# Adding the query halves in the transfer, with pair two's remainders on other engines, fewer dummy matmuls and a new order

## The chip, the cores and the metric

The kernel runs on one core of a Trainium2 chip. The metric is the device time in microseconds of one execution; the median of several runs is compared. Traces are of one profiled execution. The engines are TensorE (PE; its weight loads are PEld), VectorE (DVE), ScalarE (ACT), GpSimd (POOL) and SyncE (SP, which only issues transfers here).

## What is computed

Attention with pooled queries, then a layer of eight experts with a capacity. All inputs and outputs are float32.

```python
def _attn_ref(q, k, v):                      # q, k, v: (8, 8, 1152, 64)
    q_pool = q.reshape(B, H, S // 2, 2, D).mean(axis=3)
    scores = scale * np.matmul(q_pool, k.transpose(0, 1, 3, 2))
    scores = scores - np.max(scores, axis=-1, keepdims=True)
    attn = np.exp(scores)
    attn = attn / (np.sum(attn, axis=-1, keepdims=True) + 1e-09)
    return np.matmul(attn, v)

# x = the 4608 x 512 attention result; logits = x @ w_gate (512 x 8)
# the logits are taken in falling order: a token goes to the expert if it has none yet
# and the expert has fewer than 4608 / 8 = 576 tokens
    h = np.maximum(x[mask] @ w1[e], 0.0)
    out[mask] = h @ w2[e]
```

## The kernel before

**Work and stages.** `attention()` (line 355 on) works on 32 pairs of heads, 0 to 31. A pair has 18 steps: nine blocks of 128 keys for each of its two heads. It is followed by `experts()` (line 966 on), which the change leaves alone. The 576 queries of a head are the sums of two neighbours, so the queries come as two halves of 128 x 576 numbers (both heads of a pair on the 128 partitions), which have to be added.

**A pair's preparation.** `load` (L484) has SP fetch both query halves into QD (576 KB) and the keys into KD in two parts; `load_v` (L492) fetches VD. `split` (L557) adds the halves into QS on VectorE (L561), and makes of the scaled float32 numbers two float16 numbers each, a high part and a remainder: QH and QL of the queries, KH and KL of the keys. `values` (L615) does the same for V, into V16. ScalarE writes the high parts; VectorE writes the remainders (QL L583, KL L596, V L631), each in one instruction that scales and subtracts. For pair 0 ScalarE scales the data in place instead, and GpSimd subtracts. The scales are powers of two that `bounds` (L496) works out of the sums of absolute values (ScalarE, L502 and L506), which TensorE adds over the partitions (L511 to L516), VectorE turns into a power of two (VE, L527) and ScalarE into SC and EX (L538 on). `spread` (L599) has SP copy the parts into the operands KA, KB, QA and QB.

**The row maxima.** `max_chunk` (L635) multiplies the high parts (QH, laid out as BD, by KH) once more on TensorE into two banks, ma and mb, by turns (L654, and L664 for the ends; pair 0: L645), and VectorE takes the maximum of each bank (MX, L657). A bank is written anew when its maximum has been taken. `aug` (L692) puts the maxima into a row of QB, so that the score matmul subtracts them.

**A step.** `step` (L720): four score matmuls (sc, L737), the exponential on ScalarE (P, L740), the remainder of P against its upper half on GpSimd (PM, L744), for some steps on VectorE, and the weighted sums (av, L754), a few steps later. After a head's nine steps `evac` (L764) divides (RS, X L775). Pairs also send a piece of w1 through WB (`weights`, L432): GpSimd's queue loads it (L434), ScalarE sums its squares. At the start TensorE runs dummy matmuls into av (L877).

**What sets the order.** All instructions are put in one list, and `Cycle.plan` (L159 on) sorts it by topological order: of the items whose producers are placed, the one with the lowest number goes next, a number read from a table by the item's tag (TAU; TAU0, TAU1, TAU2 for pairs 0, 1 and 2) plus 25 for each pair. Each engine runs its own items in that order. AT holds some constants: wu, wv and wx are the dummies at three places, pd the steps of a pair whose PM goes to VectorE, pd0 and pd1 the same for the first and the last pair, lag the steps from a score to its weighted sum. SP's and GpSimd's queues issue transfers in that order too, and a transfer that has to wait holds up what stands behind it.

## Time and profile before

| what | value |
|---|---|
| median of 3 runs | 1302.52 us (1301.43 to 1305.13) |
| the profiled execution's own time | 1301.33 us |
| its span, first to last instruction | 1299.6 us |
| mean granted TensorE clock | 0.98 |
| DMA over the span | 190.83 MB, mean 147 GB/s |
| busy 200 to 300 us: PE, DVE, ACT, POOL | 95.91, 96.48, 86.05, 82.80 of 100 us |

The span splits into the start (to about 65 us), the steady stretch of pairs, the last pairs to about 810 us, and the experts. A row of a group gives the instruction by line, engine, operation and tile, its count, total or mean time. A row of the chain gives start, duration and the instruction which the end followed from. A wait reads "waiting instruction <- what ended the wait". Durations of matmuls overlap their successors.

### The profile page before, as it was taken

The page shows a single profiled execution, that of the slowest core. Times are in us where ns is not written, and L with a number is a line of the kernel's source. Part 1 is how long each engine was busy: PE and PEld are TensorE (multiplying, and loading weights), DVE is VectorE, ACT ScalarE, POOL GpSimd, SP SyncE. Part 2 cuts the span into 40 slices and gives each one's busy share as a digit, 9 for nine tenths or more (in the row PEclk, how much of TensorE's full clock was granted, in tenths as well). Part 3 has the DMA queues.
Part 4 walks back from the last instruction along what each step waited for, and adds up shares of the span by engine and source line. Part 5 has one row for each costly group of instructions (what it writes and reads, how often), then busy time and mean ns, then how long its engine had stood idle before and what let it go on. Part 6 is the DMA issues. An engine that isn't in the chain of part 4 may idle for free.

```text
span 1299.6 us, 38894 instructions
## 1 busy us (share of the span) xinstructions
PE 1215.2 (94%) x15503; PEld 869.1 (67%) x15505; DVE 1083.0 (83%) x2777; ACT 958.6 (74%) x1707; POOL 886.6 (68%) x844
## 2 busy tenths in 40 slices
PE   7889999999999999999999999979989989999998
PEld 2567777777777777777776777656655665665663
DVE  4889999999999999999999996688887888883420
ACT  4668888888888888888888886236866765767851
POOL 4658788788788778788788787244664663757541
PEclk7999999999999999999999999799988999999999
DMA  5556656557557556657557532040553435547301
GB/s 192 147 156 183 170 152 196 162 153 199 155 152 189 165 153 186 170 153 199 159 151 199 137 89 76 20 166 23 182 175 109 148 115 188 161 133 233 114 29 37
DMA packets 126754, 190.83 MB, mean 147 GB/s; under 512 B 49772, under 2 KB 85612, under 8 KB 124268
## 3 DMA queue, kind: packets, MB, share of 16 engines
q1 hardware_dynamic: 113340, 119.11, 34.5%
q0 software_dynamic: 13088, 69.21, 15.8%
q8 instruction: 121, 1.98, 0.6%
q14 instruction: 61, 0.50, 0.1%
q10 hardware_dynamic: 144, 0.02, 0.0%
HBM read 116.41 MB, written 18.87 MB: 104 GB/s over the span
## 4 chain that ended last, share of the span: by engine, by line
PE 64%; DVE 27%; issue 3%; DMA 2%; ACT 2%; POOL 0%; SPq 0%; POOLq 0%; DVEq 0%; ACTq 0%
PE sc L737 15%; PE av L754 15%; PE ph L1512 10%; PE po L1542 10%; DVE MX L657 8%; DVE QS L561 3%; PE ma L654 3%; PE mb L654 3%; DVE V L631 3%; PE av L877 1%; DVE ST L1271 1%; DVE GE L1147 1%; DMA W<-in_w_dram,widx 1%; PE av L789 1%; PE av L801 1%
## 5 line engine op out<-in xcount | busy, mean ns | idle before, releaser
L744 POOL TENSOR_TENSOR PM<-P 128x576 f16<-128x576 f32 x506 | 613.0, 1233 | 161.0 <-ACT P L740 82.8
L740 ACT ACTIVATE P<-sc,EX 128x576 f32<-128x576 f32 x576 | 412.0, 736 | 110.7 <-PE sc L737 107.0
L754 PEld LDWEIGHTS <-P 128*128 128x128 bf16 x5760 | 298.8, 98 | 65.9 <-issue 36.6
L754 PE MATMUL av<-V,P 128*128 128x65 f16 (+1 forms) x5760 | 310.2, 193 | 0.4
L754 PE MATMUL av<-V,PM 128*128 128x65 f16 x2880 | 300.3, 195 | 0.0
L754 PEld LDWEIGHTS <-PM 128*128 128x128 f16 x2880 | 265.6, 97 | 0.0
L737 PE MATMUL sc<-QB,KB 65*128 65x288 f16 (+1 forms) x1152 | 235.9, 285 | 1.3 <-DMA QB<-AU 1.3
L737 PE MATMUL sc<-QA,KA 128*128 128x288 f16 x1152 | 234.7, 285 | 1.7 <-ACT P L740 1.5
L657 DVE TENSOR_REDUCE MX<-ma 128x1 f32<-128x512 f32 x279 | 190.7, 684 | 12.4 <-PE ma L654 9.5
L657 DVE TENSOR_REDUCE MX<-mb 128x1 f32<-128x512 f32 x279 | 190.6, 683 | 4.7 <-PE mb L654 2.0
L1542 PE MATMUL po<-W2H,HX 128*128 128x512 f16 x512 | 155.8, 379 | 0.0
L1512 PE MATMUL ph<-XL,W1H 128*128 128x320 f16 (+1 forms) x512 | 148.5, 290 | 0.7 <-DVE XL L1375 0.7
L1512 PE MATMUL ph<-XH,W1H 128*128 128x320 f16 (+1 forms) x512 | 148.6, 290 | 0.2 <-ACT XH L1373 0.2
L1512 PE MATMUL ph<-XH,W1L 128*128 128x320 f16 (+1 forms) x512 | 148.5, 290 | 0.0
L737 PEld LDWEIGHTS <-KA 128*128 128x128 f16 x1152 | 103.1, 97 | 65.5 <-issue 28.1
L737 PEld LDWEIGHTS <-KB 65*128 65x128 f16 (+1 forms) x1152 | 112.4, 98 | 31.4 <-issue 1.7
L654 PE MATMUL ma<-KH,BD 128*128 128x512 f16 x279 | 105.8, 379 | 26.7 <-DVE MX L657 25.0
L1542 PEld LDWEIGHTS <-HX 128*128 128x128 f16 x768 | 70.9, 98 | 80.4 <-issue 2.6
L1512 PEld LDWEIGHTS <-W1H 128*128 128x128 f16 x1024 | 99.5, 99 | 32.2 <-issue 7.3
L654 PE MATMUL mb<-KH,BD 128*128 128x512 f16 x279 | 105.7, 379 | 6.7 <-DVE MX L657 4.0
L1564 POOL DMA_INDIRECT out_dram<-OT,idx x40 | 39.3, 983 | 106.1 <-ACT OT L1544 92.4
L1542 PE MATMUL po<-W2L,HX 128*128 128x512 f16 x256 | 97.0, 379 | 0.0
(299 smaller groups left out, 2185.8 us busy)
## 6 DMA issues: line engine op xcount, KB each, us to landing
KD<-in_kt_dram SPq DMA_DIRECT2D x64, 288.0 KB
QD<-in_qt_dram SPq DMA_DIRECT2D x32, 576.0 KB
VD<-in_v_dram SPq DMA_DIRECT2D x32, 576.0 KB
WB<-in_w_dram POOLq DMA_DIRECT2D x32, 512.0 KB, 5.3
QA<-QH SPq DMA_DIRECT2D x128, 72.0 KB
KA<-KH SPq DMA_DIRECT2D x64, 144.0 KB
KB<-KH SPq DMA_DIRECT2D x64, 144.0 KB
KA<-KL SPq DMA_DIRECT2D x64, 144.0 KB
```

Source lines behind the costliest of these rows:

```text
L561: od.add(t, "DVE", 675, lock=1, fn=lambda: nc.vector.tensor_tensor(qs, QD[n % 2][:, 0], QD[n % 2][:, 1], op=OP.add), r=[("QD", n % 2)], w= ...
L631: od.add(t + AT["vh"] + AT["vd"] * s, "DVE", 725, lock=1, fn=lambda s=s: nc.vector.scalar_tensor_tensor(V16[i][:, s, :, 0:D], VD[n % 2][:, ...
L654: od.add(t, "PE", 214, lambda: nc.tensor.matmul(m, BD[i][:, j, :], KH[i][:, 512 * c:512 * c + 512], start=True, stop=True), r=bd + [("KH", ...
L657: od.add(t, "DVE", 597, lambda: nc.vector.tensor_reduce(MX[i][:, j, c:c + 1], m, axis=AX.X, op=OP.max), r=[mk], w=[("MX", i, j, c)], tag=" ...
L737: nc.tensor.matmul(c[:, t, :288], a[i][:rows, s, ks], b[i][:rows, s, 288 * t:288 * t + 288], start=first, stop=not first)
L740: od.add(g + 0.1, "ACT", 624, lambda: nc.scalar.activation(p.rearrange("p (t q) -> p t q", t=2), c[:, :, :288], AF.Exp, scale=EX[n % 3][:, ...
L744: od.add(g + 0.2, en, dur, lock=1, fn=lambda: eng.tensor_tensor(pm, p, hi, op=OP.subtract), r=[("P32", g % NP)], w=[("PM", g % NM)], tag="pm")
L754: nc.tensor.matmul(out, w[:, qs], v, start=kb == 0 and j == 0 and y == 0, stop=kb == NKB - 1 and y == 2, skip_group_check=True)
L789: nc.tensor.transpose(m[:, 128 * z:128 * z + 128], X[u][:, 3 * q + z], ident)
L1512: nc.tensor.matmul(p, a[:, d, fs], b[:, d, qs], start=z == 0, stop=z == 11)
L1542: nc.tensor.matmul(o, a[:, z, q0:q0 + 128], b[:, z], start=z == 0 and y == 0, stop=z == 7 and y == 2)
L1564: st = nc.gpsimd.indirect_dma_start(out=out, out_offset=bass.IndirectOffsetOnAxis(ap=idx[i][:n, c:c + 1], axis=0), in_=OT[ob][:n], in_offs ...
```

## The change

**The query halves.** From pair 1 on SP loads the first half straight into QS, and GpSimd's queue then issues a transfer of the second half that adds to QS as it lands (`accum_op=OP.add`). VectorE's 31 additions go; pair 0 still adds on VectorE. QD has one buffer instead of two.

**Pair two** (n == 1). The remainders QL, KL (two) and V (two) are made as pair 0's are: ScalarE scales the data in place (five instructions), GpSimd subtracts (five). The five VectorE instructions that scaled and subtracted go.

**Dummies.** wu 30 to 10, wv 22 to 0, wx 18 to 14: 70 to 24.

**Order.** All four tables are new, and some constants. Step 14 of pair 0 has its PM on VectorE; the last pair has nine there instead of ten. Rows per engine go from 2488 to 2447 (VectorE), 725 to 759 (GpSimd), 30445 to 30353 (TensorE), 1467 to 1472 (ScalarE), 596 to 651 (SP).

```diff
-TAU = {"abs": [-49.5809, -45.8931, -41.8524], "aug": [-19.2801], "augd": [-75.843, -39.0698], "augt": [-3.7377],
+TAU = {"abs": [-47.6427, -47.0398, -38.3034], "aug": [-113.6912], "augd": [-107.9004, 5.2066], "augt": [-3.0348],
...
-AT = {"load": -12.5, "vload": -13.3, "split": -10.3, "bound": -10.3, "bq": 0.1, "bv": -0.1, "bs": 0.1, "spread": 1.6,
-      "val": -5.4, "vh": -1.4, "vd": -0.5, "mm": -3.9, "cw": 0.737, "fold0": 3.5, "fold1": 11.1, "aug": 12.8, "lag":
-      6, "np": 10, "nm": 10, "stick": 1, "nx": 3, "wu": 30, "pd": [4, 12], "wv": 22, "pd0": [], "pd1": [1, 3, 4, 5, 6,
-      7, 9, 12, 14, 16], "d1": 2.0, "cw1": 0.7, "wx": 18, "wy": 0}
+AT = {"load": -10.5, "vload": -13.3, "split": -11.0, "bound": -10.3, "bq": 0.1, "bv": -0.1, "bs": 0.1, "spread": 1.5,
+      "val": -5.4, "vh": -1.4, "vd": -0.5, "mm": -3.9, "cw": 0.709, "fold0": 3.5, "fold1": 11.4, "aug": 12.8, "lag":
+      5, "np": 10, "nm": 10, "stick": 1, "nx": 3, "wu": 10, "pd": [4, 12], "wv": 0, "pd0": [14], "pd1": [4, 5, 7, 8,
+      9, 12, 15, 16, 17], "d1": 2.0, "cw1": 0.7, "wx": 14, "wy": 0}
...
     def load(n, t):
-        od.add(t, "SP", 650, lambda: nc.sync.dma_start(QD[n % 2], qt[n]), w=[("QD", n % 2)], tag="ld",
-               late=3500 if not n else 6000)
+        if n < 1:
+            od.add(t, "SP", 650, lambda: nc.sync.dma_start(QD, qt[n]), w=["QD"], tag="ld",
+                   late=3500 if not n else 6000)
+        else:
+            od.add(t, "SP", 650, lambda: nc.sync.dma_start(QS[n % 2], qt[n][:, 0]), w=[("QS", n % 2)], tag="ldq", late=6000)
+            od.add(t, "POOL", 650, lambda: nc.gpsimd.dma_start(QS[n % 2], qt[n][:, 1], accum_op=OP.add),
+                   r=[("QS", n % 2)], w=[("QS", n % 2)], tag="qa", late=6500, lock=False)
...
-        od.add(t, "DVE", 675, lock=1, fn=lambda: nc.vector.tensor_tensor(qs, QD[n % 2][:, 0], QD[n % 2][:, 1], op=OP.add),
-               r=[("QD", n % 2)], w=[qk], tag="qs")
+        if n < 1:
+            od.add(t, "DVE", 675, lock=1, fn=lambda: nc.vector.tensor_tensor(qs, QD[:, 0], QD[:, 1], op=OP.add),
+                   r=["QD"], w=[qk], tag="qs")
...
+        if n == 1:
+            od.add(t + 2, "ACT", 665, lambda: nc.scalar.activation(qs, qs, AF.Copy, scale=QC),
+                   r=[("QH", i), ("SC", n % 3, 1)], w=[qk], tag="kd")
+            od.add(t + 3, "POOL", 1105, lambda: nc.gpsimd.tensor_tensor(QL[n % 2], qs, QH[i], op=OP.subtract),
+                   r=[qk, ("QH", i)], w=[("QL", n % 2)], tag="ql")
+        else:
...
+            if n == 1:
+                od.add(t + 4.5 + 2 * z, "ACT", 665, lambda h=h: nc.scalar.activation(KD[n % 2][:, h], KD[n % 2][:, h], AF.Copy, scale=KS),
+                       r=[("KH", i, z), ("SC", n % 3, 0)], w=[("KD", n % 2, z)], tag="kd")
+                od.add(t + 5 + 2 * z, "POOL", 1105, lambda h=h: nc.gpsimd.tensor_tensor(KL[n % 2][:, h], KD[n % 2][:, h], KH[i][:, h], op=OP.subtract),
+                       r=[("KD", n % 2, z), ("KH", i, z)], w=[("KL", n % 2, z)], tag="kl")
+                continue
...
-            if n == 0:
+            if n < 2:
```

VectorE in the middle of the pairs, before: from the row of a pair's maxima (AU) on, with the maxima (MX) of the pair after it, V's remainder and the addition.

```order
L710 TENSOR_SCALAR AU<-mb,EX_118 9x128
L657 TENSOR_REDUCE MX_140<-ma 128x1
L657 TENSOR_REDUCE MX_140<-mb 128x1
L657 TENSOR_REDUCE MX_140<-ma 128x1
L657 TENSOR_REDUCE MX_140<-mb 128x1
L631 SCALAR_TENSOR_TENSOR V_103<-VD_124,SC_113,V_103 128x9x64
L561 TENSOR_TENSOR QS_125<-QD_121 128x576
L657 TENSOR_REDUCE MX_140<-ma 128x1
L657 TENSOR_REDUCE MX_140<-mb 128x1
L657 TENSOR_REDUCE MX_140<-ma 128x1
L631 SCALAR_TENSOR_TENSOR V_103<-VD_124,SC_113,V_103 128x9x64
```

The same place of the same pair in the changed kernel:

```order
L724 TENSOR_SCALAR AU<-mb,EX_118 9x128
L671 TENSOR_REDUCE MX_139<-ma 128x1
L671 TENSOR_REDUCE MX_139<-mb 128x1
L671 TENSOR_REDUCE MX_139<-ma 128x1
L671 TENSOR_REDUCE MX_139<-mb 128x1
L645 SCALAR_TENSOR_TENSOR V_103<-VD_123,SC_113,V_103 128x9x64
L671 TENSOR_REDUCE MX_139<-ma 128x1
L671 TENSOR_REDUCE MX_139<-mb 128x1
L671 TENSOR_REDUCE MX_139<-ma 128x1
L645 SCALAR_TENSOR_TENSOR V_103<-VD_123,SC_113,V_103 128x9x64
```

The addition is gone and nothing stands in its place; V and the maxima keep their sequence.

GpSimd in the changed kernel, around one pair's load of WB and its accumulating transfer (PM is the remainder of an exponential P, by buffer); before, the same stretch held the load of WB and PM alone.

```order
L758 TENSOR_TENSOR PM_153<-P_143 128x576
L758 TENSOR_TENSOR PM_156<-P_146 128x576
L430 DMA WB<-in_w_dram 128x1024
L758 TENSOR_TENSOR PM_155<-P_145 128x576
L758 TENSOR_TENSOR PM_157<-P_147 128x576
L486 DMA QS_124<-in_qt_dram 128x576
L758 TENSOR_TENSOR PM_158<-P_148 128x576
L758 TENSOR_TENSOR PM_152<-P_142 128x576
```

The accumulating transfer comes third after the load of WB, with the PM of the next steps behind it.

TensorE at the start of the changed kernel: the last of the first ten dummies, then the scale matmuls (L512 to L517 adds the sums over the partitions, down holds constants) and pair 0's first maximum matmul; before, the fortieth dummy stood in that place.

```order
L891 MATMUL av_169<-wide,ones 128x512
L512 LDWEIGHTS down
L512 MATMUL mb<-floor,down 128x4
L515 LDWEIGHTS down
L515 MATMUL mb<-VM_126,down 128x1
L517 LDWEIGHTS down
L517 MATMUL mb<-VM_126,down 128x2
L659 LDWEIGHTS QH_89
L659 MATMUL av_168<-KH_85,QH_89 128x384
```

Thirty dummies fewer run ahead of the scale; between it and the first score matmul stand 13 instead of 22.

More of the change, by code (lines that the diff above doesn't have):

```diff
@@ new lines @@
+TAU0 = {"abk": [-40.9119, -95.4549], "abs": [-57.8076, -38.7931], "aug": [-25.919499, -1.8114], "augt": [-25.9195,
[5 rows of a table added]
+        -4.5793, 2.210901, 4.093401, 7.1828, 24.146301], "expb": [-19.224499, -17.215799, -12.648699, -7.988699,
+        0.597502, 2.906501, 4.881401, 22.6261, 22.626103], "fill": [-45.877, -97.9324, -29.1689, -79.8335, -162.9854,
+        -105.8721, -105.872099, -45.1887, -52.9623, -48.1904, -61.7411, -106.907], "fold": [-27.112598, -5.452199],
+        "kd": [-40.91187, -40.911881, -38.3778], "kh": [-40.911893, -40.911886], "kl": [-40.911869, -40.91188], "ld":
+        [-248.491, -146.5391, -216.3672], "ldv": [-106.8315], "ldw": [-45.852], "mm0": [-40.91189, -35.7719,
[9 rows of a table added]
+        4.0934, 5.0608, 24.1463], "qkb": [-19.2245, -17.2158, -12.6487, -7.9887, 0.597501, 2.9065, 4.8814, 12.1371,
+        22.626102], "ql": [-29.3401], "qs": [-99.0546], "rc": [5.859702, 25.307815], "sc": [-40.911897], "scv":
+        [-34.082899], "spr": [-40.911877, -40.911868, -40.911885, -37.9141, -34.0728, -29.340099, -40.911882, -27.638,
+        0.5975, -12.8741, -25.606, -29.340098], "vd": [-34.082896, -26.0525], "vh": [-34.082897, -34.082898], "vl":
+        [-26.052498, -26.052499], "vs": [-40.911899, -40.911898, -38.793099, -38.793098], "vsh": [-34.0829], "wsq":
[4 rows of a table added]
@@ new lines @@
+TAU1 = {"abs": [-50.5216, -56.619999, -59.249], "aug": [-0.276995], "augd": [-0.276979, -0.276977], "augt":
[6 rows of a table added]
+        -23.274099, -16.020999, -21.150099, -11.143399, -20.860099, -14.181699, -0.276998], "mre": [-27.6743, -0.277,
+        -6.541099], "qa": [-56.62], "qh": [-43.607995], "ql": [-26.054699], "sc": [-43.607998], "scv": [-24.6853],
+        "spr": [-37.964496, -33.613498, -37.964499, -43.607992, -37.2749, -17.8354, -12.4076, -15.0785, -37.964498,
+        -43.607991, -43.60799, -17.993], "vd": [-24.685297, -14.1722], "vh": [-24.685298, -24.685299], "vl":
+        [-14.172198, -14.172199], "vs": [-43.608, -43.607999], "vsh": [-43.607997]}
@@ L280, in routing_tables @@
+TAU2 = {"abs": [-43.097399, -28.5327, -26.4467], "aug": [0.298003], "augd": [0.298004, 0.298005], "augt": [0.298002],
[10 rows of a table added]
+AT = {"load": -10.5, "vload": -13.3, "split": -11.0, "bound": -10.3, "bq": 0.1, "bv": -0.1, "bs": 0.1, "spread": 1.5,
[3 rows of a table added]
 def routing_tables(nc, pool, ident, jp, scratch, do):
@@ L399, in attention @@
     KD = several(2, [128, S], F32, "KD")
-    QD = several(2, [128, 2, M], F32, "QD")
+    QD = several(1, [128, 2, M], F32, "QD")[0]
     VD = several(2, [128, 2, NKB, D], F32, "VD")
@@ L433, in weights @@
         e, z = divmod(n, 4)
-        od.add(t, "POOL", 1000, lambda: nc.gpsimd.dma_start(WB, w1[128 * e:128 * e + 128, 1024 * z:1024 * z + 1024]), w=["WB"],
+        od.add(t, "POOL", 570, lambda: nc.gpsimd.dma_start(WB, w1[128 * e:128 * e + 128, 1024 * z:1024 * z + 1024]), w=["WB"],
                tag="ldw", late=6500, lock=False)
@@ L582, in split @@
                r=[qk, ("SC", n % 3, 1)], w=[("QH", i)], tag="qh")
-        od.add(t + 2, "DVE", 728, lock=1, fn=lambda: nc.vector.scalar_tensor_tensor(
-            QL[n % 2], qs, QC, QH[i], op0=OP.mult, op1=OP.subtract),
-               r=[qk, ("QH", i), ("SC", n % 3, 1)], w=[("QL", n % 2)], tag="ql")
+        if n == 1:
[4 more added lines that the diff above has]
+        else:
+            od.add(t + 2, "DVE", 728, lock=1, fn=lambda: nc.vector.scalar_tensor_tensor(
+                QL[n % 2], qs, QC, QH[i], op0=OP.mult, op1=OP.subtract),
+                   r=[qk, ("QH", i), ("SC", n % 3, 1)], w=[("QL", n % 2)], tag="ql")
         for s in range(2):
@@ L876, in attention @@
         for _ in range(AT.get(x, 0)):
-            od.add(t, "PE", 213, lambda b=b: nc.tensor.matmul(av[b], ones, wide, start=True, stop=True), w=[f"av{b}"], tag=x)
+            od.add(t, "PE", 320, lambda b=b: nc.tensor.matmul(av[b], ones, wide, start=True, stop=True), w=[f"av{b}"], tag=x)
     for i in range(2):
```

44 lines of the change are left out of this document (13 added, 31 removed), and 96 rows, old and new, of tables (TAU, TAU0, TAU1, TAU2).

## The prediction

> **What bounds the kernel now.** I read the page's head and chain first, then the windows, then the chain and the waits inside a pair.
>
> ```profile
> span 1299.6 us, 38894 instructions
> PE 1215.2 (94%) x15503; PEld 869.1 (67%) x15505; DVE 1083.0 (83%) x2777; ACT 958.6 (74%) x1707; POOL 886.6 (68%) x844
> PE 64%; DVE 27%; issue 3%; DMA 2%; ACT 2%; POOL 0%; SPq 0%; POOLq 0%; DVEq 0%; ACTq 0%
> ```
>
> TensorE (PE) holds 64% of the chain, but VectorE (DVE) holds 27%: two engines take turns at setting the end. Where they hand over shows in the chain of waits, here around one middle pair (start, us, what), with the first and the last query addition of 26 pair periods:
>
> ```profile
> 122.25 1.69 DVE QS L561
> 290.83 1.14 DVE V L631
> 291.96 1.69 DVE QS L561
> 293.65 0.61 DVE MX L657
> 294.31 0.38 PE ma L654
> 755.85 1.69 DVE QS L561
> ```
>
> From 122.25 to 755.85 are 26 periods: (755.85 − 122.25) / 26 = 24.37 us a pair. In each, V's remainder (1.14) and the query addition QS (1.69) stand in a row between two maxima; the bank `ma` is then read late, and TensorE's matmul L654 comes late. The waits of 100 to 750 us (total us, times, longest) and TensorE's own row say how long it stands:
>
> ```profile
> PE ma L654 <- DVE MX L657: 23.4, 25, 1.1
> PEld av L789 <- DVE X L775: 5.6, 8, 1.3
> PE av L789 <- DVE X L775: 3.3, 4, 0.9
> POOL PM L744 <- issue: 71.3, 26, 2.8
> 294.31 0.38 PE L654 MATMUL ma<-KH,BD 128*128 128x512 f16 x1 [1.08 <-DVE MX L657]
> ```
>
> So 23.4 / 25 = 0.94 us a pair are lost behind V and QS, and (5.6 + 3.3) / 26 = 0.34 behind the X of VectorE. GpSimd (POOL) has a hole of 71.3 / 26 = 2.74 us a pair. The windows (us, then busy PE, PEld, DVE, ACT, POOL, then granted clock, DMA share, GB/s) give one period, one late stretch that has V but no QS, QL or KL, and the start:
>
> ```profile
> 292.00:316.40 24.40, 23.32 (x383) 18.09 (x381) 23.42 (x45) 20.84 (x38) 19.98 (x18) 1.00 0.67 180
> 781.10:804.64 23.54, 22.43 (x389) 17.87 (x386) 16.56 (x30) 14.72 (x24) 18.85 (x18) 1.00 0.28 75
> 10.00:20.00 10.00, 6.28 (x27) 2.47 (x26) 5.10 (x13) 6.53 (x12) 4.14 (x5) 0.82 0.26 78
> 20.00:30.00 10.00, 8.78 (x23) 2.56 (x25) 5.88 (x13) 3.56 (x6) 0.39 (x1) 0.50 0.64 176
> 30.00:40.00 10.00, 9.26 (x54) 4.64 (x54) 7.27 (x17) 8.01 (x16) 6.70 (x6) 0.99 0.54 149
> ```
>
> In a period VectorE is busy 23.42 of 24.40 us, TensorE 23.32: both are full, and VectorE's work is the one that can be taken away.
>
> **The change, part by part.**
>
> *The additions leave VectorE.* In the steady stretch one VectorE instruction a pair goes:
>
> ```profile
> 97.28 1.77 DVE L561 TENSOR_TENSOR QS<-QD 128x576 f32<-128x576 f32 x1
> L561 DVE TENSOR_TENSOR QS<-QD x32: 736/1768/1774, 5.8 to 755.8; 128x576 f32<-128x576 f32 x32
> L434 POOL DMA_DIRECT2D WB<-in_w_dram x32: 555/557/730, 32.0 to 802.8; - x32
> DMA to landing us min/median/max: 4.2/5.3/7.6
> 781.74 1.73 DVE L631 SCALAR_TENSOR_TENSOR V<-VD,SC,V 128x576 f16<-128x576 f32 x1
> 784.12 0.38 PE L654 MATMUL mb<-KH,BD 128*128 128x512 f16 x1 [0.42 <-DVE MX L657]
> 786.26 0.38 PE L654 MATMUL mb<-KH,BD 128*128 128x512 f16 x1 [0.56 <-DVE MX L657]
> ```
>
> The new order puts nothing in the place of QS: V stands alone between two maxima. How much of the instruction comes back? At least TensorE's measured 0.94 us. At most the whole 1.69, which the chain holds in each period: VectorE is then 23.42 − 1.77 (the longest QS) = 21.65 us busy and TensorE's own 23.32 is next. I take the 0.94 and, because a VectorE with over 2 us of air a pair should not keep `av` waiting for X, the 0.34, and a tenth for TensorE's smaller waits: 1.4, an estimate, giving a period of 24.37 − 1.4 = 23.0 us. The late stretch supports this: without QS, QL and KL it took 23.54 with 0.42 + 0.56 of waits behind a V of 1.73, so 22.56 without them, and 23.0 lies between. From 97.28 to 755.85 us stand 28 additions (the 27 from 122.25 on and the one before). 28 × 1.4 = 39.2 us; bounds 28 × 0.94 = 26.3 and 28 × 1.69 = 47.3.
>
> *What comes onto GpSimd.* Each pair brings one accumulating transfer on its queue. No row shows one; the nearest is the WB load from the same queue, 0.557 us to issue (0.730 at the longest) for 512 KB against the 288 KB here. 19.98 + 0.56 = 20.54 of 23.0 us: GpSimd still has 2.74 − 0.56 − 1.4 = 0.8 us of hole a pair. Cost 0; with all 0.730 still inside. If that cover were gone, 28 × 0.56 = 15.6 us would be due. The addition also waits for the first half, and queued behind it are PM subtractions, for which `av` on TensorE waits: a rival below. The sum is first read by ScalarE's Abs some eight exponentials later in the order, 8/18 of 23.0 = 10 us; a landing of 5.3 (7.6) plus 0.56 fits. Splitting the load does not change its bytes: 576 KB a pair as before, and one more SP issue on an engine that no chain line names. A gain is excluded: the term only adds work.
>
> *The start.* Its chain, and where the key data were ready:
>
> ```profile
> 2.28 10.72 PE av L877 x40
> 13.15 0.17 DVE VE L527
> 21.87 3.19 PE av L877 x7
> 26.71 1.82 PE av L877 x4
> 29.28 1.83 PE av L877 x6
> 31.49 0.97 PE av L877 x4
> 8.02 0.19 ACT L502 ACTIVATION_READ_ACCUMULATOR VJ<-KD 128x1 f32 x1
> ```
>
> Forty dummies hold TensorE until 13.0 us; the last Abs sum, which the scale matmuls need, was there at 8.02 + 0.19 = 8.21. Ten dummies end long before (10 × 10.72/40 = 2.7 us after 2.28). So the scale comes 13.0 − 8.3 = 4.7 us earlier. Later, 22 dummies stood before the first score matmul (21 in these rows), now 13: nine fewer at 3.19/7 = 0.456 us are 4.1 us if they are on the chain, as these rows say. That is −8.8.
>
> Pair two's remainders leave VectorE, where they sat among pair one's maxima:
>
> ```profile
> 33.80 0.76 DVE L561 TENSOR_TENSOR QS<-QD 128x576 f32<-128x576 f32 x1
> 37.09 1.63 DVE L583 SCALAR_TENSOR_TENSOR QL<-QS,SC,QH 128x576 f16<-128x576 f32 x1
> 39.57 0.80 DVE L596 SCALAR_TENSOR_TENSOR KL<-KD,SC,KH 128x576 f16<-128x576 f32 x1
> 51.04 0.82 DVE L631 SCALAR_TENSOR_TENSOR V<-VD,SC,V 128x576 f16<-128x576 f32 x1
> 50.65 1.52 ACT L740 ACTIVATE P<-sc,EX 128x576 f32<-128x576 f32 x2 [4.58 <-PE sc L737]
> 51.47 4.71 POOL L744 TENSOR_TENSOR PM<-P 128x576 f16<-128x576 f32 x4 [3.37 <-ACT P L740]
> ```
>
> Off VectorE go two QS (0.76 each), QL 1.63, two KL (0.80), two V (0.82): 6.4 us; one PM of about 0.75 (a QS-sized short form) comes on: 5.7 net. VectorE is busy 7.27 of 10 us there, so I count six tenths, −3.4 (bounds 0 and −5.7). ScalarE gets five activations at about 1.52/2 = 0.76 (3.8 us), GpSimd five subtractions at 4.71/4 = 1.18 (5.9 us). Their cover is idle time: 4.58 us on ScalarE, 3.37 us on GpSimd in front of these rows alone, and GpSimd was busy 0.39 of the ten us before 30. Uncovered, GpSimd's part beyond 3.37 would cost 2.5 us. Start in all: −12.2, between −4.7 (only the earlier scale) and −14.5.
>
> A row speaks against fewer dummies: from 20 to 30 us the granted clock was 0.50 although dummies ran there. The Trainium skill, page "TensorE: Matmul & The Clock Gate", section "Part 1: The HAM clock gate (the "warmup" mystery)", says that half clock is the default and that sustained activity of about 3.4 us lifts it; by that, leaving out busy-work would hand back some of the gain as slower matmuls. By that the sum would be the second rival's, by the row it stays. The 0.50 says that the dummies did not buy full clock there anyway.
>
> *The last pair* moves one PM of ten from VectorE to GpSimd: 0 ± 1.
>
> **Sum.** −39.2 − 12.2 = −51.4 from the profiled execution's own 1301.33 us (span 1299.6 and 1.7 around it): 1249.9. That execution lies 1.19 under the median 1302.52 of the runs shown, so 1251.1 as a median: 1251.
>
> **The rivals.**
>
> *More comes back (0.12).* VectorE's waits all go: 1.69 a pair and 14.5 at the start give 1302.5 − 47.3 − 14.5 = 1240.7, and with half of the 0.34 × 28 = 9.5 of X waits on top, 1236. Against it: TensorE's 23.32 of work a pair leaves only 1.05 us in 24.37, unless its busy time itself is stretched by waits.
>
> *The start gains nothing (0.13).* Matmuls run at 0.50 longer, or the loads (DMA share 0.64 from 20 to 30 us) set the pace: 1302.5 − 39.2 = 1263, and with a little lost again 1265.
>
> *GpSimd becomes the bound (0.08).* If each accumulating issue is held up by VectorE's work, GpSimd's 19.98 + 0.56 and a hold of 2.5 us (the hole that it now has, 2.74, less a bit) make 23.04 a pair, and any more is paid in full; half a us over gives 28 × 0.5 = 14 less gain: 1265. For it: GpSimd has little room. Against it: 32 issues took 0.555 to 0.730, none longer, beside a VectorE that is 96% busy. The Trainium skill, page "SBUF — State Buffer", section "Summary: rules for kernel authors", advises against hiding a GpSimd-issued DMA under VectorE work, since its descriptors are starved while VectorE runs in its fast modes; these 32 issues do not show it. By the page the time would be this rival's, by the rows the forecast's.
>
> *Slower: GpSimd stands for the first half (0.05).* The accumulation waits on GpSimd for SP's load into QS, which itself waits until the pair two before has let go of QS. If SP issues it late, GpSimd stands with PM behind it, then `av`. At a full landing of 5.3 us exposed, the hole left, 2.74 − 0.56 = 2.18, hides part; 3.12 a pair stick out, less the 1.4 saved: 1.72 × 28 = +48, and −12.2 at the start: 1302.5 + 36 = 1338. It decides from a stand of 2.18 + 1.4 + 12.2/28 = 4.0 us a pair. Against it: SP is on no line of the chain, and one buffer is free for most of a period.
>
> The change does what it says as far as the order goes: 31 additions less on VectorE. My forecast keeps 0.62.
>
> **How the numbers follow.** Likeliest 1251. The low end takes the first rival in nearly whole: 1237. The high end takes only the measured 0.94 a pair and only the earlier scale: 1302.5 − 26.3 − 4.7 = 1271.5, so 1272, which holds the two cases near 1265 too. Outside are the slow rival and about a tenth at the edges. A measurement of this kernel tells about 0.3% (4 us) from no change. Only the slow rival gives slower: 0.05; 0.02 for a balance of it and the gains; faster 0.93.
>
> **What would show it.** Right: no QS row on VectorE after the first, about 23.0 us from one V to that of the next pair, L654's wait for MX under 0.3 us a pair, the scale row near 8.3 us, accumulate issues near 0.56 us, GpSimd without a wait for a DMA. Wrong: PM rows released by a DMA of QS; GpSimd busy over 95% of a period; X or MX still ahead of TensorE with 1 us; a first score matmul no earlier than before; a period above 23.5 us.

## The result, and the profile after

The changed kernel is slower by 1.1%: median 1318.12 us of 4 runs (1313.03 to 1322.48) against 1303.77 of before on the same chip; ratio 1.0111 [1.0069, 1.0152]. The prediction of 1251 (1237 to 1272), with 0.93 for faster, was wrong in size and in sign. The profiled execution took 1313.03 us.

The head and the chain's shares of the page after:

```profile
span 1311.2 us, 38907 instructions
PE 1209.9 (92%) x15459; PEld 868.1 (66%) x15459; DVE 1061.4 (81%) x2741; ACT 968.4 (74%) x1712; POOL 893.8 (68%) x880
PE 67%; DVE 21%; DMA 5%; issue 3%; ACT 3%; POOL 0%; SPq 0%; POOLq 0%; DVEq 0%; ACTq 0%
```

VectorE lost 21.6 us of recorded work and 6 points of the chain; DMA gained 3. (A VectorE instruction that is held up, as shown below, is recorded as longer, so the time for which it is held counts as work.) The counts are those of the edits: 36 instructions fewer on VectorE, 36 more on GpSimd. SP issues 32 query loads as before (31 of QS and one of QD), so the additional issue of a pair is GpSimd's and not, as the prediction has it, SP's. The waits from 100 to 750 us:

```profile
POOL PM L758 <- issue: 56.0, 25, 2.6
PE ma L668 <- DMA BD<-QH: 19.2, 16, 2.5
PEld L668 <- DMA BD<-QH: 15.0, 10, 2.8
PE mb L668 <- DVE AU L724: 14.0, 9, 3.2
PE ma L668 <- DVE MX L671: 0.4, 2, 0.2
```

The wait that the change aimed at went from 23.4 to 0.4 us. Two new ones took its place: for BD, the high parts of the queries that SP copies to the maxima's operand (0.4 us before), and for AU, the row that carries the maxima (none before). The start of the chain of waits and some of its VectorE rows say more:

```profile
79.63 6.33 DVE KL L610
113.45 5.34 DMA BD<-QH
...
296.57 2.62 DVE nib L331
321.44 2.43 DVE nib L334
```

`nib`, like `scratch`, `diag` or `slots`, is a small table for the routing of the experts (L326 to L345), of which VectorE makes one or two pieces a pair in pairs 2 to 17. Before, such a piece took:

```profile
310.88 0.16 DVE L338 TENSOR_SCALAR nib<-scratch 128x16 f32<-128x16 int32 x1
```

After, in pair 11, VectorE:

```profile
344.99 0.81 DVE L610 SCALAR_TENSOR_TENSOR KL<-KD,SC,KH 128x576 f16<-128x576 f32 x1
346.19 0.49 DVE L789 TENSOR_TENSOR X<-av,RS 128x320 f32<-128x320 f32 x1
346.60 2.71 DVE L335 TENSOR_SCALAR scratch<-scratch 128x64 f32<-128x64 int32 x1
349.34 0.33 DVE L724 TENSOR_SCALAR AU<-mb,EX 9x128 f16<-9x128 f32 x1
```

and GpSimd at the same time:

```profile
343.83 1.24 POOL L758 TENSOR_TENSOR PM<-P 128x576 f16<-128x576 f32 x1 [2.08 <-issue]
345.01 0.87 POOL L486 DMA_DIRECT2D QS<-in_qt_dram  x1
345.64 3.61 POOL L758 TENSOR_TENSOR PM<-P 128x576 f16<-128x576 f32 x3
350.22 1.15 POOL L758 TENSOR_TENSOR PM<-P 128x576 f16<-128x576 f32 x1 [0.97 <-ACT P L754]
```

A run is here a row of GpSimd's instructions without a pause between them; GpSimd's hole is the pause of some 2 us that it makes in each pair. The piece starts at 346.60, inside the run that follows the accumulating issue, and ends at 349.31, 0.06 us after that run (345.64 + 3.61 = 349.25). AU stands behind it. X, which started 1.18 us behind the same issue and reads the bank av, took its usual 0.49 us. A piece is long in the same way in each of pairs 2 to 15 and in pair 17: 2.6 to 3.0 us, twice 3.79. In a late pair, where there is no such piece, AU comes 1.6 us after KL, and not 4.4:

```profile
618.13 0.81 DVE L610 SCALAR_TENSOR_TENSOR KL<-KD,SC,KH 128x576 f16<-128x576 f32 x1
619.74 0.33 DVE L724 TENSOR_SCALAR AU<-mb,EX 9x128 f16<-9x128 f32 x1
```

The first exponential of each pair (first row of P in a pair) cuts the span into periods; all in us, of one profiled execution each, with the experiments that the text below explains:

| kernel | first exp | pairs 0, 1, 2, 3 | pairs 4–18, each | pairs 19–30, each | pair 31 on |
|---|---|---|---|---|---|
| before | 32.99 | 40.39 27.08 23.59 23.48 | 24.45 | 24.19 | 494.93 |
| after | 26.04 | 37.66 35.82 28.62 26.10 | 25.37 | 23.22 | 497.78 |
| e2 | 25.97 | 38.34 35.31 27.69 23.27 | 24.27 | 23.40 | 497.94 |
| e4 | 25.93 | 39.07 30.90 28.26 24.37 | 25.38 | 24.60 | 497.68 |
| e6 | 24.92 | 37.26 35.18 28.44 23.34 | 24.17 | 23.25 | 496.76 |
| e13 | 25.35 | 37.92 34.41 28.72 22.65 | 24.24 | 23.25 | 497.97 |
| e14 | 33.38 | 43.54 27.38 23.80 30.22 | 29.53 | 28.16 | 497.66 |
| e15 | 31.89 | 40.38 25.49 31.45 23.47 | 24.59 | 24.97 | 499.56 |
| e16 | 25.49 | 37.46 29.03 27.92 23.19 | 24.37 | 23.22 | 500.56 |

After against before: −6.95 at the first exponential, −2.7 in pair 0, then +8.7, +5.0 and +2.6 in pairs 1 to 3, +13.8 in pairs 4 to 18 (15 × 0.92), −11.6 in pairs 19 to 30 (12 × 0.97), +2.85 behind: +11.7, the difference of the spans (11.6) but for rounding. So the late pairs do what was forecast, and the earlier ones give back more.

### The profile page after: what moved, and what is told of

Its sections match the earlier page's. It is cut to its first block, busy times and chain, and to the rows that moved or that the text cites. A ratio compares the mean times of both kernels' runs of the same rounds, so it can differ in the third digit from the quotient of the medians.

```text
span 1311.2 us, 38907 instructions
## 1 busy us (share of the span) xinstructions
PE 1209.9 (92%) x15459; PEld 868.1 (66%) x15459; DVE 1061.4 (81%) x2741; ACT 968.4 (74%) x1712; POOL 893.8 (68%) x880
## 3 DMA queue, kind: packets, MB, share of 16 engines
q0 software_dynamic: 17552, 78.36, 20.6%
## 4 chain that ended last, share of the span: by engine, by line
PE 67%; DVE 21%; DMA 5%; issue 3%; ACT 3%; POOL 0%; SPq 0%; POOLq 0%; DVEq 0%; ACTq 0%
PE sc L751 17%; PE av L768 14%; PE ph L1526 11%; PE po L1556 10%; PE mb L668 4%; PE ma L668 4%; DMA BD<-QH 3%; DVE MX L671 2%; ACT P L754 2%; DVE KL L610 2%; DVE ST L1285 1%; DMA KD<-in_kt_dram 1%; DVE PM L758 1%; PE av L803 1%; DMA XG<-XB 1%
## 5 line engine op out<-in xcount | busy, mean ns | idle before, releaser
L758 POOL TENSOR_TENSOR PM<-P 128x576 f16<-128x576 f32 x506 | 594.7, 1231 | 167.0 <-ACT P L754 102.1
L754 ACT ACTIVATE P<-sc,EX 128x576 f32<-128x576 f32 x576 | 409.4, 737 | 117.7 <-PE sc L751 105.4
L768 PE MATMUL av<-V,P 128*128 128x65 f16 (+1 forms) x5760 | 304.5, 193 | 0.4
L768 PE MATMUL av<-V,PM 128*128 128x65 f16 x2880 | 295.7, 195 | 0.0
```

Source lines behind the costliest of these rows:

```text
L754: od.add(g + 0.1, "ACT", 624, lambda: nc.scalar.activation(p.rearrange("p (t q) -> p t q", t=2), c[:, :, :288], AF.Exp, scale=EX[n % 3][:, ...
L758: od.add(g + 0.2, en, dur, lock=1, fn=lambda: eng.tensor_tensor(pm, p, hi, op=OP.subtract), r=[("P32", g % NP)], w=[("PM", g % NM)], tag="pm")
L768: nc.tensor.matmul(out, w[:, qs], v, start=kb == 0 and j == 0 and y == 0, stop=kb == NKB - 1 and y == 2, skip_group_check=True)
```

## The experiments

### First series: what makes the early pairs long

**e1**, the changed kernel again.

> The changed kernel once more, as the control for the next runs. Theory A (the small VectorE instructions that build the routing tables, one or two a pair in pairs 2 to 17, stand in a run of GpSimd subtractions and last 2.6 to 3.8 us instead of 0.2, and the addition's gain is eaten there): the same picture again, 25.4 us a pair in pairs 4 to 18 and 23.3 in pairs 19 to 30, and table instructions of about 2.7 us. Theory B (the loss of the first pairs is chance, above all the one KL instruction of 6.42 us at 79.55): the KL instruction is near 0.8 us in this run and the time about 7 us lower than 1313.

1315.92 us (7 runs), ratio 1.0102 [1.0062, 1.0142]; periods 25.56 and 23.30. The loss is no accident.

**e2**: the routing pieces ahead of QL and KL, some 3.4 us ahead of the issue instead of 1.6 us behind it, and so outside the run.

```diff
-"tab": [-53.4983]
+"tab": [-59.5]
```

> The changed kernel with one number altered, the priority of the table instructions (tab, -53.5 to -59.5): they then stand ahead of QL, where GpSimd has its hole, instead of right ahead of AU. Theory A: each lasts 0.2 us, pairs 4 to 18 fall from 25.4 to the 23.3 us of the later pairs, 15 x 2.1 = 31 us less, and some 3 in pairs 2 and 3: 1318 - 33 = about 1285. Theory C (the early pairs are slow because BD, SP's queue or the new order as a whole is late there, and the long table instructions only fill time that is lost anyway): within 6 us of the changed kernel, 1312 to 1322.

1299.65 (12 runs), 0.9967 [0.9944, 0.9990]. Every piece is short again, as this group of VectorE's shows (100 to 500 us: count, total us, mean ns):

```profile
L331 DVE TENSOR_SCALAR nib<-scratch 128x16 f32<-128x16 int32 x4 | 0.7, 164 | 0.0
```

Pairs 4 to 18 went from 25.37 to 24.27, about half of the 2.1 us a pair that I had expected. The instructions are the same; only what they met is gone.

**e3**: before, with the pieces right ahead of AU, as after has them.

```diff
-"tab": [-56.3881]
+"tab": [-54.8]
```

> The kernel before with the same kind of number altered the other way (tab, -56.4 to -54.8): its table instructions then stand right ahead of AU, at a time when GpSimd starts a run of subtractions. Theory A: they last about 2.4 us there, AU comes 2 us later in some 16 pairs, and the time rises by 16 x 1 to 16 x 2 us: 1320 to 1335. Theory C: the place of instructions of 0.2 us in an order does not matter, within 4 us of 1303.

1303.77 (10 runs), 0.9992 [0.9969, 1.0015]; most pieces took 0.33 to 0.46 us, and none waited for the whole run. The place alone does nothing.

**e4**: e2 with the whole load and VectorE's additions back (two buffers of QD; the additions get places of their own in the tables).

```diff
-nc.sync.dma_start(QS[n % 2], qt[n][:, 0])
-nc.gpsimd.dma_start(QS[n % 2], qt[n][:, 1], accum_op=OP.add)
+nc.sync.dma_start(QD[n % 2], qt[n])
...
+nc.vector.tensor_tensor(qs, QD[n % 2][:, 0], QD[n % 2][:, 1], op=OP.add)
```

> The changed kernel with the table instructions moved as in the run before, and the query halves added on VectorE again from pair 1 on (QD with two buffers, loaded whole; the addition right behind V's first remainder as in the kernel before). What the accumulating transfer is worth by itself: by the prediction 1.4 us a pair over 28 pairs, so 39 us above the run before, about 1324. If the new order by itself had removed the waits (the addition then lasts 0.75 us and not 1.77), only 0.5 us a pair: 14 us above, about 1299.

1322.53 (4 runs), 1.0126 [1.0088, 1.0163]: 22.9 us over e2, and 1.1 to 1.2 us a pair (25.38 and 24.60 against 24.27 and 23.40). So the query edit is a gain once the pieces are out of its way, 22.9 us where 39 had been expected. That e4 came out near the expected 1324 is luck: e2, from which the 39 were counted, had been put at 1285.

e4 says one thing more. It has all of the change but the query edit, with the pieces moved, and it is 1.3% slower than before (18.7 us), where the fewer dummies and pair two's remainders had been forecast to save 12.2. Its traced execution is some 22.5 us longer than that of before: −7.1 at the first exponential, −1.3 in pair 0, +9.4 in pairs 1 to 3, +14.0 in pairs 4 to 18, +4.9 in pairs 19 to 30 and +2.8 behind. And TensorE waits for BD (100 to 750 us), though no transfer adds to QS in this kernel:

```profile
PE ma L662 <- DMA BD<-QH: 21.8, 17, 2.2
PEld L662 <- DMA BD<-QH: 13.1, 8, 2.5
```

These are 34.9 us, as in after (19.2 + 15.0). So the waits for BD came with the new order, and not with the accumulating transfer. The additions' place in the new order is one choice of mine (nearly half of them last 1.70 us there, the others some 0.75), so a better place might make e4 somewhat faster.

### Second series: where the accumulating issue stands

**e5**: after, the issue one subtraction earlier, at the end of a run, ahead of GpSimd's hole.

```diff
-"qa": [-57.7231]
+"qa": [-59.4]
```

> The changed kernel with one number altered: the accumulating transfer (qa, -57.7 to -59.4) is issued one subtraction earlier on GpSimd, in its hole and not at the head of the run of three subtractions that follows; the table instructions stay right ahead of AU. Theory A1 (it is the accumulating issue at the head of the run that chains the subtractions, 1.38 us long at a spacing of 1.105, so that a table instruction gets in only behind the last; the kernel before, whose runs are not headed so, let it in after 0.33 us): table instructions of 0.2 to 0.4 us, no KL of 6.42 us, 1318 - 16 (as in the run with the table moved) - 6 = about 1296. Theory A2 (any run of three does it): table instructions stay at 2.7 us, the time within 5 us of 1316.

1400.24 (4 runs), 1.0737 [1.0695, 1.0778], for an expected 1296. The pieces are short (0.14 to 0.55 us, one of 1.07), but 130 to 700 us now holds

```profile
PE ma L668 <- DMA BD<-QH: 65.6, 20, 4.1
PEld L668 <- DMA BD<-QH: 26.5, 8, 4.3
```

and in one pair GpSimd's and SP's rows and TensorE's first maximum matmul read

```profile
422.19 0.86 POOL L486 DMA_DIRECT2D QS<-in_qt_dram  x1
423.75 1.21 SPq L596 DMA_DIRECT2D BD<-QH  x1
429.17 0.38 PE L668 MATMUL ma<-KH,BD 128*128 128x512 f16 x1 [2.31 <-DMA BD<-QH]
```

With the addition issued 1.6 us ahead of BD's second copy, that copy is first used 5.4 us after its issue here and 5.4 to 7.0 in the other pairs; before, it was 2.4 to 3.5, all but once without a wait, and where TensorE waited for it, it was 3.4 to 5.5 in after, with the addition 1.75 us behind it, and 3.2 to 5.1 in e4, with none. So an addition issued ahead of the copy makes it later, and one behind it makes no difference that these runs show. That the two transfers share something is inferred from the order of issue alone.

**e6**: e2 with BD's second copy ahead of the copy of QL in SP's queue, so that it no longer waits for VectorE's QL.

```diff
-"bdd": [-158.905, -45.4607]
+"bdd": [-158.905, -158.9]
```

> The kernel with the table instructions moved (1299.65), and SP's second copy of QH into BD put right behind the first, not behind the copy of QL, which waits for VectorE. Theory D (TensorE's first maximum matmul waits for BD because SP's queue stands behind QL; these waits were 14.7 + 8.1 us over 15 pairs): some 1 us a pair over 27 pairs comes back, 1275 to 1285. Theory E (BD is late because the scale and QH are late; the place in the queue does not matter): within 4 us of 1299.65.

1292.05 (4 runs), 0.9905 [0.9872, 0.9939]: faster than both kernels, but short of the expected 1275 to 1285. Pairs 10 and 14 stayed at 28.85 and 28.79; without them pairs 4 to 18 would be at 23.45. In pair 10 GpSimd, VectorE and TensorE read

```profile
282.86 0.87 POOL L486 DMA_DIRECT2D QS<-in_qt_dram  x1
283.49 9.64 POOL L758 TENSOR_TENSOR PM<-P 128x576 f16<-128x576 f32 x8
```
```profile
287.55 3.47 DVE L645 SCALAR_TENSOR_TENSOR V<-VD,SC,V 128x576 f16<-128x576 f32 x1
```
```profile
291.68 0.58 PE L668 MATMUL ma<-KH,BD 128*128 128x512 f16 x1 [1.89 <-DVE MX L671]
```

Here GpSimd's run behind the issue was not broken after three subtractions but went on, and V came into it. The row of eight subtractions hides a pause of 0.11 us behind the sixth, which ended at 290.40; V ended 0.62 us after that. The windows behind TensorE's stall of 1.89 us (the third number from the end is the granted clock):

```profile
290.00:292.00 2.00, 0.32 (x1) 0.10 (x1) 2.00 (x3) 1.06 (x2) 1.89 (x3) 0.86 0.38 86
292.00:294.00 2.00, 2.00 (x28) 1.67 (x27) 1.67 (x3) 0.00 (x0) 1.13 (x2) 0.50 0.59 135
294.00:296.00 2.00, 2.00 (x28) 1.63 (x27) 1.29 (x2) 0.71 (x2) 0.00 (x0) 0.78 0.46 118
```

The stall costs more than itself, since the clock falls to 0.50: the three windows are short of full clock by 0.28, 1.00 and 0.44 us, which is some 3.4 us at half clock.

**e7** (e6 with e5's edit) and **e8** (e7 with pair two's remainders back on VectorE).

```diff
-"qa": [-57.7231]
+"qa": [-59.4]
```

and for e8, in `split` (twice) and `values`:

```diff
-if n == 1:
+if n < 0:
...
-if n < 2:
+if n < 1:
```

> All three numbers altered: the table instructions moved, the second BD copy behind the first, the accumulating transfer one subtraction earlier. If A1 and D hold, the KL of 6.42 us is gone too: 6 to 8 us under the run with two numbers altered, 1268 to 1278. If only A1 holds: about 1292.

> As the run before, and pair two's remainders (QL, two KL, two V) made on VectorE again as in the kernel before. By the prediction these five are worth 5.7 us of VectorE and 3.4 us of time: 3 to 4 us slower than the run before, pair 0 and 1 longer. If ScalarE and GpSimd set the pace at the start instead: equal or up to 5 us faster.

1366.62 (6 runs), 1.0469 [1.0440, 1.0498], and 1380.93 (4 runs), 1.0594 [1.0545, 1.0643]. My hope that BD's earlier copy would clear the collision fell: it took 5.2 to 8.1 us to its first use. e8 is 14.3 us slower than e7, where 3 to 4 had been expected.

**e9** (after, as below) and **e10** (e6, with −55.8): the issue later, behind the subtractions.

```diff
-"qa": [-57.7231]
+"qa": [-55.0]
```

> The changed kernel with one number altered the other way: the accumulating transfer (qa, -57.7 to -55.0) is issued behind the run of three subtractions and not at its head. Theory F (BD, which TensorE waits for, and the accumulating transfer share the DMA engines: issued 1.75 us behind BD's second copy, BD is in use 4 to 5 us after its issue; issued 1.9 us ahead of it, 5.4 to 7; without one, 3.0): BD is in use at 3 to 4 us, and its waits fall under 0.5 us a pair. Theory A1: table instructions of 0.2 to 0.4 us and no KL of 6.42 us. Both: 1316 - 16 - 6 - 8 = about 1286. If only a place ahead of a run matters to VectorE and BD is late for other reasons: about 1294.

> The kernel with the table instructions moved and the second BD copy behind the first (1292.05), with the accumulating transfer two subtractions later (-55.8). Theory F and A1: no KL of 6.42 us (6 us) and less of BD's wait (0.5 us a pair): 1275 to 1283. If the sum of the query halves, some 2.2 us later, then makes ScalarE's Abs and with it the scale and BD late: 1292 or above.

1319.80 (4 runs), 1.0112 [1.0088, 1.0136], and 1310.84 (12 runs), 1.0066 [1.0040, 1.0092]; the gains expected of both missed, and of e10's two cases the worse one came, in which Abs waits. Pieces and pair 1 are good (28.04 in e9), but the KL that in after starts 0.02 us ahead of the issue (344.99 above) and takes 0.81 us now meets a subtraction and takes 1.79 in most pairs, and ScalarE's Abs waits for the sum (from 540 to 770 us 11.1 us in 6 places in e9, 7.3 us in 5 in e10). In e10 V is also held for 3.8 to 4.2 us in six pairs. Late pairs (19 to 30): 25.13 and 24.96.

### Third series: the start

**e11**: e6 with pair two's remainders on VectorE (n == 1; e8's diff of `split` and `values`). **e12**: e6 with the 46 dummies back (with places for them in a table).

```diff
-"wu": 10, "wv": 0, "wx": 14
+"wu": 30, "wv": 22, "wx": 18
...
```

> The kernel with the table instructions moved and the second BD copy behind the first (1292.05), with pair two's remainders on VectorE again. By the prediction slower by 3.4 us (0 to 5.7): 1292 to 1298. In the run with the transfer earlier pair 0 took 10.5 us more with them on VectorE (50.10 for 39.56): if that holds here, 1300 to 1303.

> The same kernel (1292.05) with the 70 dummies of the kernel before: 40 ahead of the scale, 23 before the first score matmul, 6 later. By the prediction the fewer dummies are worth 4.7 + 4.1 us: 1301, the first exponential 8.8 us later (near 34). The rival (the start gains nothing, since dummies only fill time and raise the clock): within 4 us of 1292.

e11: 1303.57 (10 runs), 1.0003 [0.9978, 1.0028], 11.5 us over e6. The two traced executions lie 20.3 us apart, 13.1 of it in pair 0 (50.39 for 37.26). e12: 1312.66 (4 runs), 1.0088 [1.0061, 1.0115], 20.6 over e6, where 9 had been expected. Its first exponential comes 6.2 us later (31.11), but pair 4 begins only 2.6 us later (151.8 for 149.1); much of the rest is in pairs 10, 14 and 18 (29.80, 31.45 and 28.47 us; in the first two V is held for 3.5 us), so how much of the 20.6 is the dummies' own stays open.

### Fourth series: is it the accumulating form, and when does the hold end?

**e13**: after, the second half transferred without `accum_op`, which leaves out the sum of the halves.

```diff
-nc.gpsimd.dma_start(QS[n % 2], qt[n][:, 1], accum_op=OP.add)
+nc.gpsimd.dma_start(QS[n % 2], qt[n][:, 1])
```

> The changed kernel with the second half of each query tile transferred plainly over the first (same place in GpSimd's order, same bytes, no addition: the sum of the halves is left out). Theory (it is the accumulating form of the issue, at the head of a run of GpSimd's subtractions, that keeps VectorE's small routing instructions and the first KL instruction waiting to the end of the run): the issue is 0.56 us instead of 0.87, no routing instruction of pairs 4 to 18 exceeds 0.6 us, pair 1's long KL instruction of 6.4 us is under 2 us, pairs 4 to 18 fall from 25.4 to some 24.2 us, and the time to 1290 to 1300 us. Rival (any issue by GpSimd at the head of the run does this): routing instructions stay at 2.6 to 3.8 us and the time within 6 us of 1315. On the transfers: if an addition in flight takes more than a plain transfer of the same bytes, landing is well under the 5.6 us, and TensorE's waits for BD from QH fall too.

1291.49 (5 runs), 0.9910 [0.9877, 0.9943]. The issue is 576 ns (865 in after), and the piece of pair 11 is short, at the same place behind the same run:

```profile
332.57 0.58 POOL L486 DMA_DIRECT2D QS<-in_qt_dram  x1
333.17 3.46 POOL L758 TENSOR_TENSOR PM<-P 128x576 f16<-128x576 f32 x3
```
```profile
334.17 0.25 DVE L335 TENSOR_SCALAR scratch<-scratch 128x64 f32<-128x64 int32 x1
```

So, at this place, the pieces are held by the accumulating form. Two points missed: pair 1's KL, which came 0.16 us behind the issue, was still 4.41 us, and TensorE's waits for BD did not fall (35.7 us from 100 to 750, 34.2 in after).

**e14**: before's own order, with the query edit alone (split load, one buffer of QD, `accum_op`; pairs 1 and 2 have places of their own), issued behind the first subtraction after GpSimd's hole. **e17** is the same kernel once more.

```diff
+"ldq": [-72.0], "qa": [-57.7]
...
```

> The kernel before, in its own order, with one edit: query halves of pairs 1 to 31 added by the second transfer, issued by GpSimd behind the first of the four subtractions after its hole; the start, the dummies and pair two's remainders stay. Theory: the issue stands inside the run and not at its head, so the routing instructions stay under 0.6 us; MX waits for QS go, the issue is some 2 us behind the second BD copy, which so lands at most 1 us late; but KL is no longer sheltered by the place. Gain 0.3 to 0.9 us a pair over 28 pairs: 1279 to 1296 us. Rival (the addition in flight costs the copies of BD or TensorE's supply what it saves, wherever it is put): 1300 or more, with TensorE waiting for BD in most pairs.

> A second look at the old order with the addition behind the first of the four subtractions. Theory: the V instruction that follows AU takes 6.5 to 7.1 us in most pairs again and ends within 0.7 us of the end of GpSimd's run; time 1420 to 1440 us. Rival (chance of one job): V under 1.3 us.

1428.47 (4 runs), 1.0952 [1.0908, 1.0995]; e17 1426.76 in one run. The first expectation missed by 130 us, by the mechanism that it had named: it looked only at the pieces and KL. GpSimd, and then VectorE:

```profile
331.16 0.87 POOL L490 DMA_DIRECT2D QS<-in_qt_dram  x1
331.76 4.75 POOL L750 TENSOR_TENSOR PM<-P 128x576 f16<-128x576 f32 x4
336.18 0.84 POOL L434 DMA_DIRECT2D WB<-in_w_dram  x1
336.77 4.72 POOL L750 TENSOR_TENSOR PM<-P 128x576 f16<-128x576 f32 x4
```
```profile
331.14 0.17 DVE L335 TENSOR_SCALAR nib<-scratch 128x16 f32<-128x16 int32 x1
334.49 0.68 DVE L663 TENSOR_REDUCE MX<-mb 128x1 f32<-128x512 f32 x1
335.08 7.03 DVE L637 SCALAR_TENSOR_TENSOR V<-VD,SC,V 128x576 f16<-128x576 f32 x1
```

The piece, started 0.02 us ahead of the issue, goes free; maxima go free at any time (0.67 to 0.69 us); V comes in the middle and ends 0.62 us behind the run's end at 341.49. It took over 4 us in 26 of the pairs; its mean was 1.09 us before.

**e15**: as e14, with the issue one subtraction earlier (`"qa": [-58.5]`).

> As the run before, but the issue stands at the head of the four subtractions, at the end of GpSimd's hole. Theory: the routing instruction, which stands some 1.5 us after the head there, is held to the end of the run (2.5 to 3.5 us long in pairs 4 to 17 instead of 0.16), though nothing else of the new order is in this kernel; BD is late too, since the issue comes within 1 us of its second copy (some 2 to 4 us a pair): 1310 to 1370 us. Rival (the holding needs the new order, where the routing instruction is right ahead of AU): routing instructions under 0.6 us.

1326.33 (4 runs), 1.0189 [1.0153, 1.0225]. The place turned out to be ahead of the hole, not behind it:

```profile
337.51 0.86 POOL L490 DMA_DIRECT2D QS<-in_qt_dram  x1
340.33 4.62 POOL L750 TENSOR_TENSOR PM<-P 128x576 f16<-128x576 f32 x4 [1.95 <-issue]
```
```profile
341.64 1.14 DVE L340 TENSOR_SCALAR diag<-scratch 128x64 f16<-128x64 int32 x1
```

GpSimd stands still for 1.95 us after the issue, and a piece in the next run waits for one subtraction (1.14 us, as the same piece did in before), not for four. My expectation of 2.5 to 3.5 fell; what it says is that the hold ends when GpSimd stands still. BD is late, as in e5 (39 us of waits from 130 to 700), though in e14, where the issue comes behind the copy, TensorE does not wait for it.

**e16**: e6, with the issue for pair 4 alone (n == 4, issued during pair 1) put behind the work that follows it.

```diff
-tag="qa"
+tag="qb" if n == 4 else "qa"
+"qb": [-51.0]
```

> The version with the routing instructions and BD's second copy moved, and one more edit: pair four's addition alone is issued behind the work that follows it in GpSimd's order, so that GpSimd waits right after the issue (before the 10.6 us wait in pair 1). Theory (an accumulating issue keeps GpSimd's share of the common access from the issue until GpSimd first stands still, and a VectorE instruction that comes in between waits to that end): with nothing behind the issue the 6.42 us KL instruction of pair 1 falls under 2 us, pair 1 from 35.2 to some 30 us, later pairs stay, and the time is 4 to 7 us under 1292: 1285 to 1288 us. Rival (the 6.4 us come from the half clock and the IOTA there, not from the issue): KL stays above 4 us and the time within 3 us of 1292.

1286.20 (4 runs), 0.9839 [0.9775, 0.9904], the lowest median of all. It lies 5.9 us under e6, as expected, but the intervals of the two overlap and their traced executions are equally long (spans 1287.9 and 1287.4), so the gain in time is not shown. What the trace shows is pair 1. In after, its KL stood in this run:

```profile
79.39 0.86 POOL L486 DMA_DIRECT2D QS<-in_qt_dram  x1
80.04 3.58 POOL L758 TENSOR_TENSOR PM<-P 128x576 f16<-128x576 f32 x3
...
83.98 1.36 POOL L758 TENSOR_TENSOR PM<-P 128x576 f16<-128x576 f32 x1
```
```profile
79.55 6.42 DVE L610 SCALAR_TENSOR_TENSOR KL<-KD,SC,KH 128x576 f16<-128x576 f32 x1
```

and in e16, the same subtractions without an issue ahead of them:

```profile
77.00 5.09 POOL L758 TENSOR_TENSOR PM<-P 128x576 f16<-128x576 f32 x4 [1.83 <-PE sc L751]
...
83.77 0.84 POOL L486 DMA_DIRECT2D QS<-in_qt_dram  x1
88.72 2.25 POOL L758 TENSOR_TENSOR PM<-P 128x576 f16<-128x576 f32 x2 [4.10 <-ACT P L754]
```
```profile
78.37 1.61 DVE L610 SCALAR_TENSOR_TENSOR KL<-KD,SC,KH 128x576 f16<-128x576 f32 x1
```

Pair 1 went from 35.18 to 29.03, and pair 4 begins 6.0 us earlier; pairs 4 to 18 (some 3 us) and the stretch behind the pairs (3.8 us) took longer in that execution. e4, without any such issue, has the same KL at 1.61 us too, and pair 1 at 30.90.

**e18**: e14 without `accum_op` (e13's diff), so again without the sum of the halves.

> The old order with the second query half transferred plainly at that same place, behind the first of the four subtractions (the sum of the halves is left out; bytes, queue and place are the same). Theory (it is the accumulating form that holds VectorE): no V instruction exceeds 2 us, mean near 0.9 to 1.1, pairs 4 to 18 at 23.2 to 23.9 us instead of 29.5, and 1270 to 1290 us, which is then what an addition for nothing would be worth in the old order. Rival (any issue inside the run does it): V at 6 us again and 1400 or more.

1356.98 (4 runs), 1.0414 [1.0342, 1.0485]: 71 us better than e14 and 67 to 87 worse than my theory. V is long in 13 pairs, about half as many as in e14, as here, behind an issue of 0.57 us at 250.31:

```profile
254.24 6.72 DVE L637 SCALAR_TENSOR_TENSOR V<-VD,SC,V 128x576 f16<-128x576 f32 x1
```

So a plain issue inside a run can do it too, in 13 pairs for the 26 of the accumulating form. Up to 500 us, a V that came 3.87 to 3.93 us behind the issue took 4.5 to 6.8 us, one that came at 4.39 to 4.40 took 1.3, and one at 4.35 took 6.29: an instant decides that I can't name. Why the plain form leaves the pieces of e13 alone stays open too.

## Why the prediction was wrong, point by point

The prediction came to −51.4 us. Before, e1, e2 and e4 were measured side by side, and between them they take the change apart (differences of medians, us):

| part | measured | forecast |
|---|---|---|
| all but the query edit, pieces moved (before to e4) | +18.7 | −12.2 |
| the query edit (e4 to e2) | −22.9 | −39.2 |
| the pieces behind the issue (e2 to e1, the changed kernel) | +16.3 | 0 |
| sum (before to e1) | +12.1 | −51.4 |

**The additions leave VectorE (−39.2): mechanism right, size too large.** TensorE's wait for MX went (23.4 to 0.4 us). Pairs 19 to 30, which have no routing pieces, take 23.22 us, forecast 23.0; undoing the edit costs 1.1 to 1.2 us a pair (e4), forecast 1.4, and 22.9 us in all.

**What comes onto GpSimd (0): this step failed.** It read "Cost 0; with all 0.730 still inside", and it weighed only GpSimd's own time against GpSimd's hole. That sum held: the issue took 0.865 us for the estimated 0.56, GpSimd still waits 2.2 us a pair (56.0 / 25), and the addition lands in time. What it left out is who waits for GpSimd. From the issue to GpSimd's next pause, VectorE's instructions with two inputs in the on-chip memory and its small pieces wait to the end: 2.6 to 3.8 us in pairs 2 to 15 and 17, 6.4 once in pair 1. Moving the pieces (e2) returned 16 us; with no issue in front of that KL, pair 1 is 6 us shorter (e16). The prediction's own rows held a sign of this: the same addition took 0.74 to 0.76 us in the first four pairs and 1.77 in the other 28, and the prediction did not ask why. In the trace of before, a subtraction of GpSimd starts at 291.87, 0.02 us ahead of the addition (291.89), and lasts to 293.03; the addition ends at 293.66. By these, the third rival, a bound by GpSimd, had the right engine and the wrong victim: GpSimd is not full, VectorE waits. The Trainium skill, page "SBUF — State Buffer", section "Who interferes with whom", says that a VectorE instruction with two on-chip inputs, or a `tensor_scalar` in a fast mode, contends with GpSimd, and that the first to issue keeps the port for the whole instruction while a `tensor_reduce` never contends on this chip. The traces agree on who is held and who is not, and differ in how long: behind an issue the hold lasted over up to five subtractions and a second issue (e14), not one instruction. I had used that page for the opposite direction, an issue held up by VectorE; after's 31 issues, 0.83 to 0.94 us each, show nothing of it.

**The new order (put at nothing): this failed too.** The prediction said of it only "The new order puts nothing in the place of QS", and its sum has no term for the four new tables. From pair 1 on, e4's traced execution loses some 31 us against that of before. With the new tables TensorE waits for BD, 0.4 us before and 34.2 after, and e4 shows the same waits (34.9) without the transfer. Which of the table's numbers makes BD late was not singled out; putting its second copy earlier (e6) brought 7.6 us and left 30.8 us of these waits, of 40.6 in e2.

**The sum lands in time: right.** Apart from one wait at the start (2.7 us in after), Abs waits for it only in e9 and e10, where the issue was put later.

**The start (−12.2): the terms came, and were not kept.** The first exponential came 6.95 us earlier and pair 1 began 9.7 us earlier. Fewer dummies are worth 6.2 us at the first exponential (forecast 8.8) and 2.6 at the start of pair 4 (e12), pair two's remainders 11.5 in this order (forecast 3.4; bounds 0 to 5.7, too narrow). But pairs 1 to 3 gave 16.4 us back. Of it 6 is pair 1's held KL (e16), 3 the piece in pair 3 (e2). Even in e16 pairs 1 and 2 take 29.03 and 27.92, and in e4 30.90 and 28.26, before 27.08 and 23.59: why the new order is slower there was not tried. The lower clock that the second rival feared does not mark the start: after reads 0.83 over the first 40 us and e6, with the same dummies, 1.00, and their first exponentials lie 1.1 us apart.

**The slower rival** (GpSimd stands for the first half) did not happen: no PM row waits for a transfer of QS. My 0.05 was for one mechanism; the way it did go slower was not in the list. Of the signs given, "a period above 23.5 us" came true in pairs 4 to 18, and pointed at the early pairs at once.

What stays open is why the new order by itself is slower: BD's waits, two pairs with a held V, and pairs 1 and 2 are seen in the traces, but not each priced.
